# Moving the output-weight transfers four places down an in-order queue, and reordering the last iterations, in a two-problem decode attention kernel

## The chip, the cores and the metric

One core of one Trainium2 chip. The metric is the device time of one execution in microseconds (us); medians of several runs are given. A profiled execution is a run that was recorded; its "span" (first to last instruction) is mostly 1.2 to 2 us shorter than the time of the same run. The "granted clock" is the share of full speed at which TensorE was let run, as the profile gives it.

## The reference, cut to what matters

Two independent attention decodes (A and B) with the same shapes, each followed by an output projection:

```python
B, Sq, D = 2, 1, 576
Hq, Hkv, Sk, Dh = 32, 16, 16384, 128
W = 4096                                   # only the last W positions count
q = (x @ wq) -> (B, Hq, 1, Dh)
k, v = k_cache[:, :, Sk-W:], v_cache[:, :, Sk-W:]      # two query heads share a kv head
p = softmax(q k^T * Dh**-0.5);  o = p v
out = o.reshape(B, Sq, Hq*Dh) @ wo         # wo: (4096, 576)
# the outputs of A and B are concatenated on the last axis; all bf16
```

Per problem the K and V windows are 33.6 MB each and wq and wo 4.7 MB each, and every byte is used once. Nothing can be reused, so the kernel is a stream of weights and caches through the core.

## The kernel before

K and V come in slabs of 4096 KB: one slab is one batch row and four kv heads. Slabs 2G and 2G+1 (the two batch rows) make group G; there are NG = 8 groups (NSLAB = 16 slabs of K and 16 of V). The slabs pass through a ring of four slots. The wo rows of one group are a stripe of 1152 KB, in one of two buffers (`wob`). All loads are issued by SyncE, in the order of one list:

```python
        stream = []
        for t in range(NSLAB + LAG):              # LAG = 3
            if t < NSLAB:
                stream.append(("K", t))
            if t >= LAG:
                i = t - LAG
                if i % 2 == 0 and i // 2 < NG - 2:
                    stream.append(("W", i // 2))  # stripe of group G, ahead of V slab 2G
                stream.append(("V", i))
        stream.append(("W", NG - 2))
        stream.append(("W", NG - 1))
```

So the order is K0 K1 K2 K3 W0 V0 K4 V1 K5 W1 V2 K6 V3 K7 W2 V4 and so on. What a load waits for before it is issued:

```python
        def issue(key):
            kind, i = key
            if kind == "W":
                ...                               # (cut)
                sl = i % 2
                deps = [proj_op[i - 2]] if i >= 2 else []   # the buffer's last reader
                ...                               # (cut)
            r = slot_of[key]
            prior = uses[r][:uses[r].index(key)]
            deps = [last_reader[prior[-1]]] if prior else first_deps[r]  # K: transpose of slab t-2; V: PV of slab i-2
```

The iterations (t is the K slab in work; X is VectorE's transpose of half a K slab, S the score matmuls on it, PV the matmul of the probabilities with V; evac is VectorE's work on the result of a PV, dg the selection matmul that rearranges a group's result, pick what VectorE takes from it for the projection, E the output):

```python
        for t in range(NSLAB + LAG):
            i = t - LAG
            ...                                   # (cut: Gc, Gs, Gd, Gp, the groups in work)
            if live:                              # t < NSLAB
                make_X(t, 0); make_S(t, 0)
            if 0 <= i - 1 and t <= NSLAB: make_evac(i - 1)
            if Gp is not None and not last: make_pick(Gp)   # Gp = (t - 6) // 2, t even
            if Gc is not None: make_max(Gc)                 # Gc = (t - 2) // 2, t even
            ...                                   # (cut: rsum, pT of group (t - 3) // 2, t odd; Tm)
            if live:
                make_X(t, 1); make_S(t, 1)
                ...
            ...                                   # (cut: nM, sums, dg)
            if Gp is not None and not last:
                make_proj(Gp)                     # projection of group Gp with its wo stripe
                ...                               # (cut: E, at the end of a problem)
            if Gc is not None: make_bias(Gc)      # bias, then exp of the group on ScalarE
            if last: filler(4)
            if i >= 0:
                make_PV(i)
                if t >= NSLAB: make_evac(i)
        filler(3)
        make_proj(NG - 2); make_dg(NG - 1); make_pick(NG - 1)
        filler(3)
        make_proj(NG - 1); make_E(NPROB - 1)
```

The calls append to one program per engine, and each engine runs its program in order. The projection of group G-2 is in iteration t = 2G + 2, behind the second half of that iteration's scores. `filler` is a few matmuls on TensorE whose result nobody reads; they are there to keep its clock up.

## Time and profile before

| | before |
|---|---|
| time, median of 3 runs | 380.42 us (380.27 to 382.86) |
| span of the profiled run (which took 382.6 us) | 381.4 us |
| HBM to SBUF | 153.1 MB in 94.3% of the engines' time |
| transfers, 34 to 340 us | 416 GB/s |
| last bytes land | between 370 and 371 us |
| VectorE / TensorE busy | 56% / 62% |

The first line to look at is the rate row of the page: GB/s in 40 equal slices of 9.5 us.

```profile
GB/s 337 433 440 433 424 430 428 442 430 423 417 448 440 423 426 213 446 440 437 438 347 440 437 416 308 399 440 433 416 353 424 430 437 438 440 430 433 379 331 0
```

Leaving out the first and the last three, the slices are at 399 to 448, except four: 213, 347, 308 and 353. A kernel that has to bring in 153 MB and is otherwise at its full rate loses there what it never gets back. The windows view gives a hole its size. Its columns are the window, its length, busy time and number of instructions of TensorE, of its weight loads, VectorE, ScalarE and GpSimd, then the granted TensorE clock, the DMA engines' share and GB/s:

```profile
34.00:340.00 306.00, 195.00 (x998) 46.31 (x710) 194.11 (x107) 35.45 (x57) 15.45 (x56) 0.84 0.97 416
144.00:154.00 10.00, 7.49 (x61) 2.14 (x46) 4.31 (x2) 4.05 (x7) 1.06 (x3) 0.93 0.59 228
234.00:242.00 8.00, 6.12 (x58) 1.86 (x44) 3.68 (x2) 3.42 (x5) 1.06 (x3) 1.00 0.53 196
```

Over 306 us the mean is 416; the two holes shown are at 228 and 196 GB/s. The Trainium skill gives the ceiling of sixteen ports as 435 GB/s ("DMA: Bandwidth & Descriptors", section "Where 436 GB/s comes from"), and the undisturbed stretches of this trace run at 432 to 442, so the stream has little more to give than the holes. The timeline of SyncE's queue shows what stands at the end of a hole (start, length, engine and line, operation, destination and source):

```profile
119.80 0.54 SPq L369 DMA_DIRECT2D ring<-in_A_k_cache_dram  x1
149.53 0.33 SPq L353 DMA_DIRECT2D wob<-in_A_wo_dram  x1
149.91 0.54 SPq L369 DMA_DIRECT2D ring<-in_A_v_cache_dram  x1
150.49 0.61 SPq L369 DMA_DIRECT2D ring<-in_B_k_cache_dram  x1
151.54 0.54 SPq L369 DMA_DIRECT2D ring<-in_A_v_cache_dram  x1
162.56 0.54 SPq L369 DMA_DIRECT2D ring<-in_B_k_cache_dram  x1
```

From 119.80 to 149.53 us nothing is issued. Then a wo stripe goes out, and a V and a K follow at once: they had been ready, and stood behind the stripe. The Trainium skill says that any semaphore wait of a transfer takes place on the sequencer that issues it, before dispatch ("DMA: Bandwidth & Descriptors", section "Anatomy of one DMA — SWDGE (gpsimd) path"); that section is about GpSimd's transfers, but SyncE's queue agrees, as these 29.7 us without an issue show. The waits view of the queue has the stripes' line first (line waited for, us in total, times, longest):

```profile
SPq L353 <- PE tb L478: 134.3, 5, 30.2
```

134 us of waiting in five waits. The view names the small transpose on line 478, which is the next instruction after the projection on TensorE; the wait in the program is for the projection. In steady state, the distance between groups shows the pace; these are the first transposes of slabs 8, 10, 12 and 14 on VectorE:

```profile
174.04 4.45 DVE L424 STREAM_TRANSPOSE xt<-ring 128x4096 f32<-128x4096 f32 x1 [5.57 <-DMA ring<-in_B_k_cache_dram]
...
217.83 4.45 DVE L424 STREAM_TRANSPOSE xt<-ring 128x4096 f32<-128x4096 f32 x1 [3.08 <-DMA ring<-in_B_k_cache_dram]
...
262.60 4.45 DVE L424 STREAM_TRANSPOSE xt<-ring 128x4096 f32<-128x4096 f32 x1 [5.45 <-DMA ring<-in_B_k_cache_dram]
...
306.18 4.45 DVE L424 STREAM_TRANSPOSE xt<-ring 128x4096 f32<-128x4096 f32 x1 [4.39 <-DMA ring<-in_B_k_cache_dram]
```

They are 43.8, 44.8 and 43.6 us apart. The bytes of one group (four slabs and a stripe, 17.96 MB) would need 41.5 us at 433 GB/s.

Last, the end of the kernel, from the last scores on (in brackets: how long the engine had been idle, and what ended that):

```profile
345.20 0.17 DVE L511 TENSOR_REDUCE ssum<-tb 128x2 f32<-128x8 f32 x1 [5.68 <-PE tb L508]
...
350.84 1.21 DVE L458 TENSOR_REDUCE mx<-st 128x2 f32<-128x1024 f32 x1
...
357.40 1.42 ACT L488 ACTIVATE pR<-st,bias 128x512 bf16<-128x512 f32 x1 [25.44 <-DVE bias L481]
...
362.41 2.31 DVE L497 STREAM_TRANSPOSE pT<-pR 128x2048 bf16<-128x2048 bf16 x1 [1.58 <-ACT pR L488]
...
365.98 3.60 PE L527 MATMUL ot<-ring,pT 128*32 128x512 bf16 x32
...
370.99 1.91 PE L527 MATMUL ot<-ring,pT 128*32 128x512 bf16 x32
...
375.64 0.70 PE L555 MATMUL tb<-oR,selx 128*128 128x256 f32 x2
...
377.50 0.28 PE L596 MATMUL pj<-wob,oP 128*2 128x288 bf16 x1 [0.51 <-DVE oP L571]
...
380.15 0.32 SPq L610 DMA_DIRECT2D out_dram<-out_sb  x1
```

The row sums (of group 6) that follow the last scores on TensorE are read at 345.20, the maximum over the scores starts only at 350.84, exp at 357.40, and the probabilities are transposed (L497) until 364.7. The last two PVs (L527) come after that, the last one at 370.99, and the final projection at 377.50. The max is late because it stands behind the evacuation of PV 12 on VectorE, and the bias behind the projection of group 5 on TensorE.

### The profile page before, as it was taken

The numbers are of one execution on the slowest core, as the hardware profiler recorded it, in microseconds if no ns is written. First come the engines' busy times: TensorE is split into PE (matmuls) and PEld (weight loads), VectorE is DVE, ScalarE is ACT, GpSimd is POOL, SyncE is SP. The second block draws the span as 40 slices with busy tenths as digits, with TensorE's granted clock in tenths as the row PEclk, the third lists the DMA queues.
The fourth block names the chain that finished last, engine by engine and source line by source line (L and its number), as shares of the span: only waits on it lengthen the run. The fifth ranks groups of instructions, "written<-read, shape, count | busy, mean of one in ns | idle before, by whom it ended". The sixth has DMA issues, their size and how long they took to land.

```text
span 381.4 us, 2626 instructions
## 1 busy us (share of the span) xinstructions
PE 236.0 (62%) x1299; PEld 58.6 (15%) x937; DVE 212.2 (56%) x138; ACT 44.7 (12%) x77; POOL 22.0 (6%) x82
## 2 busy tenths in 40 slices
PE   0381887386546278582757768762775848754677
PEld 0110111012111112120111211110121201201122
DVE  0203889468475492907657192934839084764253
ACT  1002000500050002200050000500041000500500
POOL 3001000100100001000010001000010000000000
PEclk9997798879989968887996768888798877988769
DMA  8999999999999995999989997999989999999980
GB/s 337 433 440 433 424 430 428 442 430 423 417 448 440 423 426 213 446 440 437 438 347 440 437 416 308 399 440 433 416 353 424 430 437 438 440 430 433 379 331 0
DMA packets 6659, 153.26 MB, mean 402 GB/s; under 512 B 748, under 2 KB 888, under 8 KB 1272
## 3 DMA queue, kind: packets, MB, share of 16 engines
q1 hardware_dynamic: 6628, 153.10, 94.3%
q8 instruction: 8, 0.13, 0.1%
q14 instruction: 3, 0.02, 0.0%
q10 hardware_dynamic: 20, 0.01, 0.0%
HBM read 153.10 MB, written 0.00 MB: 401 GB/s over the span
## 4 chain that ended last, share of the span: by engine, by line
DMA 50%; DVE 22%; PE 18%; issue 7%; ACT 1%; SPq 1%; POOL 0%; DVEq 0%
DMA ring<-in_A_k_cache_dram 25%; DMA ring<-in_B_k_cache_dram 25%; DVE xt L424 13%; PE st L450 5%; PE st L242 5%; PE pj L596 2%; PE pj L242 2%; DVE oR L549 2%; DVE mx L458 2%; PE ot L527 2%; DVE tmp L548 2%; ACT pR L488 1%; DVE pT L497 1%; DVE oP L571 1%; DVE tmp L564 1%
## 5 line engine op out<-in xcount | busy, mean ns | idle before, releaser
L450 PE MATMUL st<-xt,zq 128*128 128x512 bf16 x256 | 124.1, 485 | 109.1 <-DVE xt L424 109.1
L424 DVE STREAM_TRANSPOSE xt<-ring 128x4096 f32<-128x4096 f32 x32 | 141.6, 4431 | 49.8 <-DMA ring<-in_A_k_cache_dram 27.0
L242 PE MATMUL st<-xt,zq 128*128 128x512 bf16 x256 | 122.6, 479 | 0.0
L488 ACT ACTIVATE pR<-st,bias 128x512 bf16<-128x512 f32 x32 | 40.0, 1417 | 251.4 <-DVE bias L481 251.4
L450 PEld LDWEIGHTS st<-xt,zq 128*128 128x128 bf16 x256 | 29.4, 115 | 234.1 <-DVE xt L424 125.9
L527 PE MATMUL ot<-ring,pT 128*32 128x512 bf16 x512 | 32.3, 396 | 0.0
L481 DVE SCALAR_TENSOR_TENSOR bias<-vmask,tb,offm 128x4 f32<-128x4 f32 x8 | 1.8, 225 | 43.1 <-PE tb L478 43.1
L511 DVE TENSOR_REDUCE ssum<-tb 128x2 f32<-128x8 f32 x8 | 1.3, 162 | 37.4 <-PE tb L508 37.4
L497 DVE STREAM_TRANSPOSE pT<-pR 128x2048 bf16<-128x2048 bf16 x8 | 18.4, 2304 | 2.3 <-ACT pR L488 2.3
L416 POOL TENSOR_TENSOR zq<-qs,bmask 128x64 bf16<-128x64 bf16 x32 | 8.7, 294 | 168.3 <-PE st L242 152.8
L596 PE MATMUL pj<-wob,oP 128*2 128x288 bf16 x63 | 17.3, 305 | 0.5 <-DVE oP L571 0.5
L242 PE MATMUL pj<-wob,oP 128*2 128x288 bf16 x63 | 17.3, 306 | 0.0
L549 DVE TENSOR_REDUCE oR<-tmp 128x128 f32<-128x512 f32 x16 | 16.6, 1038 | 0.6
L548 DVE SCALAR_TENSOR_TENSOR tmp<-ot,rsb,dmask 128x512 f32<-128x512 f32 x16 | 11.5, 720 | 8.0 <-PE ot L527 8.0
L527 PEld LDWEIGHTS ot<-ring,pT 128*32 128x32 bf16 x512 | 12.5, 99 | 15.6 <-issue 5.6
L252 PE MATMUL tb<-ident_b,pR 8*128 8x8 bf16 x9 | 0.7, 199 | 15.7 <-DVE pR L213 15.7
L275 PE MATMUL ot<-ring,pT 128*32 128x512 bf16 x36 | 8.9, 477 | 2.2 <-DMA ring<-in_B_wq_dram 1.7
L458 DVE TENSOR_REDUCE mx<-st 128x2 f32<-128x1024 f32 x8 | 9.7, 1213 | 0.0
L488 ACT ACTIVATION_READ_ACCUMULATOR pR<-st,bias 128x1 f32 x32 | 9.0, 281 | 0.0
L242 PE MATMUL pj<-ring,pT 128*32 128x512 bf16 x36 | 8.7, 467 | 0.0
L213 DVE TENSOR_TENSOR pR<-tmp,hmask 8x1152 bf16<-8x1152 bf16 x1 | 1.3, 1347 | 12.7 <-DMA tmp<-in_B_x_dram 12.7
L555 PE MATMUL tb<-oR,selx 128*128 128x256 f32 x16 | 6.1, 466 | 3.3 <-DVE ssum L511 3.3
(57 smaller groups left out, 61.0 us busy)
## 6 DMA issues: line engine op xcount, KB each, us to landing
ring<-in_A_k_cache_dram SPq DMA_DIRECT2D x8, 4096.0 KB, 29.4
ring<-in_A_v_cache_dram SPq DMA_DIRECT2D x8, 4096.0 KB, 32.0
ring<-in_B_k_cache_dram SPq DMA_DIRECT2D x8, 4096.0 KB, 27.2
ring<-in_B_v_cache_dram SPq DMA_DIRECT2D x7, 4096.0 KB, 27.4
ring<-in_A_wq_dram SPq DMA_DIRECT2D x1, 4608.0 KB, 13.6
ring<-in_B_wq_dram SPq DMA_DIRECT2D x1, 4608.0 KB, 24.0
wob<-in_A_wo_dram SPq DMA_DIRECT2D x4, 1152.0 KB, 15.8
wob<-in_B_wo_dram SPq DMA_DIRECT2D x3, 1152.0 KB, 5.3
```

The source lines that it names most:

```text
L242: return e.add_instruction(mybir.InstMatmult(name=nc.get_next_instruction_name(), engine=mybir.EngineType.PE, ins=[e.lower_ap(mv_), e.lowe ...
L275: last = e.matmul(o, wt, mv_, start=first, stop=True, skip_group_check=True)
L416: last = e.tensor_tensor(dst, src, msk, ALU.mult)
L424: Xop[(t, jh)] = dve(lambda e: e.transpose(xt[:, jh, :].bitcast(FP32).rearrange("p (kp x kt) -> p x kp kt", kp=2, kt=2), ring[:, r, jh * H ...
L450: last = e.matmul(ob, wt, mv_, start=first, stop=True, skip_group_check=True)
L458: ch[(G, "max")] = dve(lambda e: e.tensor_reduce(mx[:], st[:, :].rearrange("p (x t) -> p t x", t=2), AX.X, ALU.max), [Sop[(2 * G + 1, 1)]] ...
L488: last = e.activation(pR[:].rearrange("p (x k) -> p k x", k=4)[:, kv, :], st[:, :].rearrange("p (x t) -> p t x", t=2)[:, kv % 2, :], ACTF.Exp,
L497: pT_op[G] = dve(lambda e: e.transpose(pT[:, v, :].rearrange("p (w j q) -> p j w q", w=4, q=8), pR[:].rearrange("p (j w q) -> p j w q", w= ...
L527: last = e.matmul(OTB[32 * c:32 * c + 32, :], pT[:, v, base + 32 * c:base + 32 * c + 32], ring[:, r, jj * 128:(jj + 4) * 128], start=rd == ...
L548: evac_op[i] = dve(lambda e: e.scalar_tensor_tensor(tv, o, rsb[:, v, b:b + 1], dm, ALU.mult, ALU.mult), deps, "ev%d" % i)
L549: ch[(G, "red%d" % b)] = dve(lambda e: e.tensor_reduce(oR[:, b, :], tmp[:].rearrange("p (j d) -> p d j", j=4), AX.X, ALU.add), [evac_op[i] ...
L596: e.matmul(PJ[0], wt, wob[:, v, j, 0:NH], start=start and j == 0, stop=True, skip_group_check=True)
```

## The change

The intent: let a stripe never be what the queue waits for, by queueing it one group later (ahead of the even V slab of the following group), and let the chain max, bias, exp, transpose of the last group follow its last scores directly.

```diff
                 i = t - LAG
-                if i % 2 == 0 and i // 2 < NG - 2:
-                    stream.append(("W", i // 2))
+                if i % 2 == 0 and 0 < i // 2 < NG - 1:
+                    stream.append(("W", i // 2 - 1))
                 stream.append(("V", i))
@@ (cut: the loop now ends with t = NSLAB - 1 = T; its conditions for later t are dropped)
+            if t == T:
+                make_max(NG - 1)
+                make_pick(Gd)
             if i >= 0:
                 make_PV(i)
-                if t >= NSLAB:
-                    make_evac(i)
+        i = T - LAG
+        make_Tm_pe(NG - 1)
+        make_nM(NG - 1)
+        make_evac(i)
+        make_bias(NG - 1)
+        make_PV(i + 1)
+        make_evac(i + 1)
+        make_proj(NG - 3)
+        make_dg(NG - 2)
+        make_pick(NG - 2)
+        make_rsum(NG - 1)
+        make_pT(NG - 1)
+        make_sums(NG - 1)
+        filler(4)
+        make_PV(i + 2)
+        make_evac(i + 2)
+        make_PV(i + 3)
+        make_evac(i + 3)
         filler(3)
         make_proj(NG - 2)
         make_dg(NG - 1)
```

The stream becomes K5 W0 V2 K6 V3 K7 W1 V4 and so on. Bytes and matmuls are the same as before.

More of the change, by code (lines that the diff above doesn't have):

```diff
@@ L614, in build_kernel @@
             make_Z(t)
-        for t in range(NSLAB + LAG):
+        T = NSLAB - 1
+        for t in range(NSLAB):
             i = t - LAG
             odd = t % 2 == 1
-            live = t < NSLAB
             Gc = (t - 2) // 2 if not odd and t >= 2 else None
@@ L622, in build_kernel @@
             Gp = (t - 6) // 2 if not odd and t >= 6 else None
-            if Gc is not None and Gc >= NG:
-                Gc = None
-            if Gs is not None and Gs >= NG:
-                Gs = None
-            last = t == NSLAB + LAG - 1
-            if live:
-                make_X(t, 0)
-                make_S(t, 0)
-            if 0 <= i - 1 and t <= NSLAB:
+            make_X(t, 0)
+            make_S(t, 0)
+            if i >= 1:
                 make_evac(i - 1)
-            if Gp is not None and not last:
+            if Gp is not None:
                 make_pick(Gp)
@@ L641, in build_kernel @@
                 make_Tm_pe(Gc)
-            if live:
-                make_X(t, 1)
-                make_S(t, 1)
-                if t + 2 < NSLAB:
-                    make_Z(t + 2)
+            make_X(t, 1)
+            make_S(t, 1)
+            if t + 2 < NSLAB:
+                make_Z(t + 2)
             if Gc is not None:
@@ L652, in build_kernel @@
                 make_dg(Gd)
-                if Gd == NG - 2:
-                    make_pick(Gd)
-            if Gp is not None and not last:
+            if Gp is not None:
                 make_proj(Gp)
@@ L660, in build_kernel @@
                 make_bias(Gc)
-            if last:
-                filler(4)
+            if t == T:
+                make_max(NG - 1)
+                make_pick(Gd)
             if i >= 0:
                 make_PV(i)
-                if t >= NSLAB:
-                    make_evac(i)
+        i = T - LAG
[16 more added lines that the diff above has]
+        make_evac(i + 3)
         filler(3)
```

## The prediction

> **What bounds the kernel now.** The transfers. In stretches without a stall (34 to 146, 154 to 190, 198 to 234, 242 to 278, 286 to 346 us; windows view) 432 to 442 GB/s arrive. The Trainium skill ("DMA: Bandwidth & Descriptors", section "Where 436 GB/s comes from") gives 435 GB/s as the ceiling of the sixteen ports; this trace agrees. The 153 MB at 433 GB/s take 354 us (my division) of the 381.4 us span. The rest:
>
> 1. Four holes: in 144-154, 190-198, 234-242 and 278-286 us the rate is 228, 346, 196 and 318 GB/s. Against 433 that is 4.7 + 1.6 + 4.4 + 2.1 = 12.8 us lost.
> 2. The end: the last bytes land at about 370.3 us, 11 us before the end.
> 3. A start of 2 to 3 us.
>
> **Why the holes.** In the timeline of the SyncE queue every hole ends with the issue of a wo stripe (149.5, 192.9, 238.2, 281.4 us), with a V, a K and a V right after it: the queue is in order, and the stripe held them back. The stripe of group G waits for the projection of G-2, at the end of iteration 2G+2, when only one K slab (9.7 us) is still in flight.
>
> **What the change moves.** Bytes and matmuls stay equal. The stripe is queued two transfers later, behind K(2G+5), when that projection is long done. The next waits in that queue (a V for a PV, a K for a transpose) come, as I count it, 15 to 20 us before their transfer's turn. So I expect no new hole, and the stripe still lands before its projection.
>
> Would compute bind? In VectorE's timeline two iterations take about 39 us where they hardly wait for a transfer (129.3 to 168.3; 306.2 to 345.4); one group's transfers take 17.96 MB / 433 GB/s = 41.5 us. DMA still binds, by 2 to 3 us. Groups (first transposes at 174.0, 217.8, 262.6, 306.2) were 43.6 to 44.8 us apart and should be 41 to 42.
>
> **The end.** Before, the last scores end at 344.9, exp starts at 357.4, pT ends at 364.7, and the last two PVs follow. Reordered, exp should start about 6 us after the scores (max 1.2, pool operations, PV 1.9, nM, bias), so pT is done before the last V lands. Estimate: K15 lands at 312, scores end at 331, pT at 345, last V cut at 353, last byte at 357.5 (370.3 less 12.8). What remains is part of evac, projection 6, dg and pick 1.9, projection 7 with its output 3.9: the end is 6 to 8 us after the last byte, not 11. TensorE will idle waiting for V15, so the last matmuls may run at granted clock 0.50 (the trace shows it after idle stretches, as "TensorE: Matmul & The Clock Gate", section "What's actually happening", says); projection 6 would take 3.9 instead of 2.0 us.
>
> **Sum.** 12.8 us of holes and 3 to 5 us of tail: 380.4 - 15.5 = about 365 us. Range 361.5 to 370. Faster by over 2%: 0.93; within 2%: 0.065; slower by over 2%: 0.005.
>
> **What would show it.** No slice of the rate row under about 400 GB/s between first and last; no long wait of a stripe before its issue; group distance 41 to 42 us; last byte near 357.5; exp of the last group within about 7 us of its scores.
>
> **What would make it wrong.** Jitter in the 39 us compute chains that two K slots don't absorb, so that small holes appear; another wait taking the stripe's place in the queue; cold matmuls or a late last stripe (it waits for projection 5, now later on TensorE) in the tail.

## The result, and the profile after

| | before | after |
|---|---|---|
| time, median of 4 runs | 381.34 us (380.27 to 382.86) | 368.30 us (366.13 to 370.06) |
| ratio | 1 | 0.9652 (95% interval 0.9587 to 0.9718) |
| span of the profiled run | 381.4 us | 364.9 us |
| transfers, 34 to 340 us | 416 GB/s | 431 GB/s |
| last bytes land | between 370 and 371 us | between 359 and 360 us |
| from there to the end | about 11 us | about 5.5 us |

Ratios are the mean time of one kernel's runs over that of the other's runs of the same rounds, so not quite the ratio of the medians quoted. The profiled run of after is the fastest of its four (366.13 us), and that of before was a slow one (382.6 us), so the two spans differ by more (16.5 us) than the medians (13.0 us); why the others are up to 4 us slower is taken up below.

The rate row of after:

```profile
GB/s 324 449 432 417 445 418 445 420 442 427 433 417 453 413 453 392 451 435 432 427 418 449 413 449 408 449 427 438 424 422 436 427 438 419 441 431 431 413 415 128
```

Between the first slice and the last ones none is below 392. The same windows:

```profile
34.00:340.00 306.00, 202.55 (x1100) 49.83 (x796) 200.65 (x119) 39.73 (x66) 17.32 (x63) 0.86 1.00 431
144.00:154.00 10.00, 6.76 (x54) 1.91 (x43) 8.26 (x5) 5.01 (x8) 0.58 (x2) 0.87 1.03 443
234.00:242.00 8.00, 3.94 (x16) 0.77 (x8) 7.96 (x5) 1.57 (x4) 0.20 (x1) 1.00 1.01 434
```

431 over the whole stretch, and the former holes cannot be told from the rest. The queue:

```profile
118.86 0.54 SPq L369 DMA_DIRECT2D ring<-in_A_k_cache_dram  x1
119.44 0.59 SPq L353 DMA_DIRECT2D wob<-in_A_wo_dram  x1
125.79 0.54 SPq L369 DMA_DIRECT2D ring<-in_A_v_cache_dram  x1
139.19 0.53 SPq L369 DMA_DIRECT2D ring<-in_B_k_cache_dram  x1
147.24 0.54 SPq L369 DMA_DIRECT2D ring<-in_A_v_cache_dram  x1
```

The stripe is issued in the same microsecond as the K slab ahead of it: it no longer waits, and the next V waits instead, at 125.79, for a PV. That wait costs nothing, since V3, K7 and a stripe, issued before, are still in flight then (K6 has just landed, and K7 lands 20 us later). The waits view has the stripes' line with one wait left, that of the last stripe for projection 5, in the tail:

```profile
SPq L369 <- PE ot L527: 86.4, 12, 9.0
...
SPq L353 <- PE pj L242: 11.2, 1, 11.2
```

The pace, at the same four transposes:

```profile
168.14 4.45 DVE L424 STREAM_TRANSPOSE xt<-ring 128x4096 f32<-128x4096 f32 x1 [3.71 <-DMA ring<-in_B_k_cache_dram]
...
209.78 4.45 DVE L424 STREAM_TRANSPOSE xt<-ring 128x4096 f32<-128x4096 f32 x1 [4.99 <-DMA ring<-in_B_k_cache_dram]
...
251.43 4.45 DVE L424 STREAM_TRANSPOSE xt<-ring 128x4096 f32<-128x4096 f32 x1 [2.26 <-DMA ring<-in_B_k_cache_dram]
...
293.08 4.45 DVE L424 STREAM_TRANSPOSE xt<-ring 128x4096 f32<-128x4096 f32 x1 [2.39 <-DMA ring<-in_B_k_cache_dram]
```

41.6 to 41.7 us apart, which is what the bytes alone take (17.96 MB at 431 GB/s are 41.7 us). VectorE now waits 2.3 to 5.0 us for each of these slabs: it is the side with time to spare. The end:

```profile
330.93 0.17 DVE L511 TENSOR_REDUCE ssum<-tb 128x2 f32<-128x8 f32 x1 [5.68 <-PE tb L508]
...
331.21 1.20 DVE L458 TENSOR_REDUCE mx<-st 128x2 f32<-128x1024 f32 x1
...
336.13 1.41 ACT L488 ACTIVATE pR<-st,bias 128x512 bf16<-128x512 f32 x1 [18.82 <-DVE bias L481]
...
341.14 2.31 DVE L497 STREAM_TRANSPOSE pT<-pR 128x2048 bf16<-128x2048 bf16 x1 [0.45 <-ACT pR L488]
...
344.49 3.60 PE L527 MATMUL ot<-ring,pT 128*32 128x512 bf16 x32 [1.69 <-DMA ring<-in_B_v_cache_dram]
...
357.13 0.28 PE L596 MATMUL pj<-wob,oP 128*2 128x288 bf16 x1 [0.81 <-DMA wob<-in_B_wo_dram]
...
359.19 0.70 PE L555 MATMUL tb<-oR,selx 128*128 128x256 f32 x2
...
361.05 0.28 PE L596 MATMUL pj<-wob,oP 128*2 128x288 bf16 x1 [0.51 <-DVE oP L571]
...
363.69 0.32 SPq L610 DMA_DIRECT2D out_dram<-out_sb  x1
```

The maximum starts at 331.21, within 0.3 us of the row sums; exp at 336.13; the transpose is done at 343.4, and PV 14 waits for its V slab (L527 at 344.49, released by a DMA). What is left after the last bytes is projection 6, the selection matmul (L555), the pick, projection 7 and the store.

### The profile page after: what moved, and what is told of

Read it like the earlier page. It is cut to its first block, busy times and chain, and to the rows that moved or that the text cites. A ratio compares the mean times of both kernels' runs of the same rounds, so it can differ in the third digit from the quotient of the medians.

```text
span 364.9 us, 2628 instructions
## 1 busy us (share of the span) xinstructions
PE 230.3 (63%) x1297; PEld 57.4 (16%) x937; DVE 211.7 (58%) x138; ACT 44.8 (12%) x77; POOL 21.9 (6%) x82
## 4 chain that ended last, share of the span: by engine, by line
DMA 60%; DVE 23%; PE 7%; issue 6%; ACT 1%; SPq 1%; POOL 0%
DMA ring<-in_B_k_cache_dram 31%; DVE xt L424 14%; DMA ring<-in_A_k_cache_dram 14%; DMA wob<-in_B_wo_dram 8%; DMA ring<-in_B_wq_dram 7%; DVE oR L549 2%; PE st L450 2%; DVE mx L458 2%; DVE pT L497 2%; PE st L242 2%; PE pj L242 1%; ACT pR L488 1%; DVE tmp L548 1%; PE pj L596 1%; DVE oP L571 1%
## 5 line engine op out<-in xcount | busy, mean ns | idle before, releaser
L450 PE MATMUL st<-xt,zq 128*128 128x512 bf16 x256 | 120.9, 472 | 98.3 <-DVE xt L424 98.3
L242 PE MATMUL st<-xt,zq 128*128 128x512 bf16 x256 | 119.7, 468 | 0.0
L527 PE MATMUL ot<-ring,pT 128*32 128x512 bf16 x512 | 34.1, 411 | 4.8 <-DMA ring<-in_B_v_cache_dram 4.8
L596 PE MATMUL pj<-wob,oP 128*2 128x288 bf16 x63 | 15.7, 286 | 1.3 <-DMA wob<-in_B_wo_dram 0.8
L527 PEld LDWEIGHTS ot<-ring,pT 128*32 128x32 bf16 x512 | 12.7, 100 | 22.0 <-DMA ring<-in_B_v_cache_dram 8.3
L242 PE MATMUL pj<-wob,oP 128*2 128x288 bf16 x63 | 15.8, 286 | 0.0
L275 PE MATMUL ot<-ring,pT 128*32 128x512 bf16 x36 | 8.9, 486 | 5.2 <-DMA ring<-in_B_wq_dram 4.7
L607 ACT ACTIVATE out_sb<-pj 2x288 bf16<-2x288 f32 x2 | 0.8, 399 | 58.2 <-PE pj L242 36.1
## 6 DMA issues: line engine op xcount, KB each, us to landing
wob<-in_A_wo_dram SPq DMA_DIRECT2D x4, 1152.0 KB, 30.2
```

What stands on the lines that cost most here:

```text
L242: return e.add_instruction(mybir.InstMatmult(name=nc.get_next_instruction_name(), engine=mybir.EngineType.PE, ins=[e.lower_ap(mv_), e.lowe ...
L275: last = e.matmul(o, wt, mv_, start=first, stop=True, skip_group_check=True)
L450: last = e.matmul(ob, wt, mv_, start=first, stop=True, skip_group_check=True)
L527: last = e.matmul(OTB[32 * c:32 * c + 32, :], pT[:, v, base + 32 * c:base + 32 * c + 32], ring[:, r, jj * 128:(jj + 4) * 128], start=rd == ...
L596: e.matmul(PJ[0], wt, wob[:, v, j, 0:NH], start=start and j == 0, stop=True, skip_group_check=True)
```

## The experiments

All ran beside the kernel before on the same chip; 0.5% is about what three to five rounds can tell. The theory was: (1) the holes are the queue blocked by a stripe that waits for its projection, while the transfers in flight run out; (2) the reordered tail saves some us at the end. Rivals: the tail makes most of the gain; or it is not the wait but the place of the stripe's bytes in the stream.

### Each part alone

The first part alone: only the three lines of `stream`.

> Before, with the wo stripes queued two transfers later and the old order of the last iterations. My theory (the holes are the queue blocked by a stripe that waits for a projection): the four holes vanish, X of slab 15 starts at 312 to 314 us as in the changed kernel, and the old tail of 54.5 us from there (326.8 to 381.4 in before) gives a span of 366 to 368 us: about 14 us less than before, ratio 0.962 to 0.970, 2 us behind the changed kernel. Rival (the gain is mostly the reordered tail): the span stays above 375 us.

Measured: 368.97 us median of 6 runs, ratio 0.9664 (0.9626 to 0.9703), span 367.5. The transpose of slab 15 started at 313.53, the last bytes landed between 359 and 360 us, and the end followed 8 us later. As expected, and the rival (most of the gain from the tail) falls.

The second part alone: only the lines of the loop and of the tail.

> Before, with the new order of the last iterations and the stripes where they were. My theory: the four holes stay (group distance 43 to 45 us), the last byte stays near 370.5 us, and the end follows it by 5.7 us as in the changed kernel: span about 376 us, 5 us less than before, ratio 0.984 to 0.990. Then the two parts don't add up (14 + 5 against 16.5 together), because both shorten the same tail. Rival (tail is most of the gain): span under 370 us.

Measured: 378.69 us, ratio 0.9923 (0.9887 to 0.9959), span 377.4; the rate from 34 to 340 us was 417 GB/s, so the holes stayed. The gain was smaller than expected: the end came 8 us after the last bytes (369 to 370 us), not 5.7. In the timeline, projection 6 ran at half speed; these are its first and its last matmul but one, and the selection matmul that had to wait for it:

```profile
367.40 0.40 PE L596 MATMUL pj<-wob,oP 128*2 128x288 bf16 x1 [1.32 <-DMA wob<-in_B_wo_dram]
...
370.71 0.44 PE L596 MATMUL pj<-wob,oP 128*2 128x288 bf16 x1
...
371.33 1.06 PE L555 MATMUL tb<-oR,selx 128*128 128x256 f32 x2
```

A matmul each 0.24 us instead of each 0.12: sixteen take 3.9 us instead of 2.0. This is the cold TensorE that the prediction had named as a risk. In the profiled run of the changed kernel it had not happened.

The changed kernel again, for comparison:

> The changed kernel again, as a measure for the others on this chip: 366 to 370 us, ratio 0.96 to 0.97, span 365 to 367.

Measured: 368.20 us, ratio 0.9652 (0.9616 to 0.9688), span 365.0. So the parts don't add up: in the spans, 13.9 us for the stripes and 4.0 for the order make 17.9, and together they give 16.5. These are single runs; in the medians of the times it is 12.1 and 2.4 against 12.9 together. The shortfall of 1.4 to 1.6 us is no more than one kernel's runs differ among themselves, so it is likely and not shown. In the medians, the order is worth 2.4 us without the stripes' move and 0.8 with it, which the intervals can't tell from nothing. (The profiled run of the order alone was the slowest of its six; the shortest span of the six was 375.1 us.)

### Is it the wait or the place?

One transfer later instead of four (the expectation says two), on top of the changed kernel:

```diff
-                if i % 2 == 0 and 0 < i // 2 < NG - 1:
-                    stream.append(("W", i // 2 - 1))
                 stream.append(("V", i))
+                if i % 2 == 0 and i // 2 < NG - 2:
+                    stream.append(("W", i // 2))
```

> The changed kernel with each stripe queued one transfer later than in before (right behind the even V slab), not two. My theory (a hole opens only if the data in flight run out before the projection): when the even iteration starts, V, K and one V slab (29 us) are in flight ahead of the stripe, and the projection ends after about 20 us, so one step is enough: no hole, span 364 to 367 us, ratio 0.962 to 0.970, the same as the changed kernel within 0.5%. Rival (it is the distance of two transfers, or bytes of the stripe ahead of V and K, that counts): about half of the gain, ratio 0.975 to 0.99.

Measured: 367.04 us, ratio 0.9618 (0.9576 to 0.966), span 365.0. In the queue the stripes still wait (they are issued at 148.10, 189.82, 233.00 and 274.47 us, each followed at once by a K slab that stood behind it), but one more V slab is in flight meanwhile, and the rate from 34 to 340 us is 431 GB/s (the stripes' line of the waits view, where 30.2 us was the longest wait before, and the windows view):

```profile
SPq L353 <- PE tb L478: 81.2, 4, 22.5
34.00:340.00 306.00, 203.46 (x1094) 49.84 (x795) 198.82 (x117) 37.54 (x64) 17.32 (x63) 0.85 1.00 431
```

A wait in the queue without a hole: what counts is whether the data in flight outlast it.

The stripes where they were, but the projection earlier. In even iterations, `make_proj(Gp)` moves from its old place to ahead of `make_X(t, 1)`, on top of before:

```diff
+            if Gp is not None and live:
+                make_proj(Gp)
+                if (Gp + 1) % GP == 0:
+                    make_E(Gp // GP)
             if live:
                 make_X(t, 1)
@@ (cut: the call in the old place stays for t >= NSLAB alone)
```

> Before, with the stripes where they were and the old tail, but with the projection of each even iteration moved ahead of the second half of the scores on TensorE; that half waits some 4 us for its transpose anyway. The projection then ends about 10 to 12 us after the start of the iteration instead of 20. My theory (the wait for the projection makes the hole): the stripe is issued while a K slab is still in flight, the holes shrink from 12.8 us in total to under 2 us, span 367 to 370 us, ratio 0.962 to 0.975, near the run with only the stripes moved. Rival (the place of the stripe's bytes in the stream makes the loss): holes and time as before, ratio over 0.99.

Measured: 371.40 us, ratio 0.9723 (0.9689 to 0.9757), span 370.2. The third stripe was issued at 142.61 instead of 149.53, and the windows view has no hole left:

```profile
34.00:340.00 306.00, 203.60 (x1048) 48.70 (x752) 196.74 (x112) 35.35 (x57) 15.36 (x56) 0.82 1.00 431
144.00:154.00 10.00, 5.13 (x46) 1.53 (x39) 5.32 (x4) 4.99 (x8) 1.26 (x4) 0.97 1.02 433
```

So the wait makes the loss, not the place: with the bytes in the old place and the wait shortened, the rate is that of the changed kernel. The span is just over the expected range, and that part does belong to the place: with no stripe moved behind it, the last K slab lands later (slab 15 is transposed at 315.45, against 313.53 with the stripes moved), and the old tail takes 54.7 us from there.

The wait made worse: one transfer earlier than before, ahead of the odd K slab.

```diff
+            if t >= LAG and (t - LAG) % 2 == 0 and (t - LAG) // 2 < NG - 2:
+                stream.append(("W", (t - LAG) // 2))
             if t < NSLAB:
                 stream.append(("K", t))
             if t >= LAG:
-                i = t - LAG
-                if i % 2 == 0 and i // 2 < NG - 2:
-                    stream.append(("W", i // 2))
-                stream.append(("V", i))
+                stream.append(("V", t - LAG))
```

> Before, with each stripe queued one transfer earlier (ahead of the odd K slab): the suspected wait made worse. My theory: only one V slab (9.7 us) is then in flight while the projection is 20 us away, and the K slab of the next iteration waits as well; each of the four groups from the third on takes about 54 us instead of 44, so 415 to 440 us, with holes of over 10 us each. Rival (bytes of the stripe in the wrong place): no change, 380 us.

Measured: 424.25 us, one run (so of unknown state), span 422.7. The rate row, in slices of 10.6 us:

```profile
GB/s 336 447 422 434 445 412 443 437 410 448 419 431 403 2 310 447 425 416 104 257 416 431 447 150 161 447 443 406 242 82 435 440 443 436 409 447 440 403 374 2
```

Four holes again, at the same four stripes, each now spread over two slices and worth 12.3 to 13.5 us (the missing GB/s of both against 431, times 10.6 us). The first lasts from 137 to 151 us; the groups are 54.7 us apart on average (transposes at 164.46, 219.02, 273.70 and 328.65). One slab of 9.7 us less in flight made each group some 11 us longer. Two other ways to take the wait away were not run: a third stripe buffer, and issuing the stripes from another engine's queue.

### What sets the end

In the changed kernel, projection 6 on TensorE stands between the last evacuation (done at 356.8 us) and the selection matmul (359.19), which the final projection needs. The swap (it also drops three filler matmuls):

```diff
         filler(3)
-        make_proj(NG - 2)
         make_dg(NG - 1)
         make_pick(NG - 1)
-        filler(3)
+        make_proj(NG - 2)
         make_proj(NG - 1)
```

> The changed kernel with the selection matmul and the pick of the last group ahead of projection 6 on TensorE, and without the filler between them. My theory of the tail (the last stripe pair and the last evac are ready at 357.1 and 356.8 us, and projection 6 delays the selection matmul from 356.9 to 359.2): the end comes 1.5 to 2 us earlier, span about 363 us. Rival (the landing of the last stripe binds): less than 0.5 us.

Measured: 367.13 us, ratio 0.9613 (0.9577 to 0.9649), span 363.4: 1.6 us less in the profiled runs, 1.1 in the medians of the same chip (367.13 against 368.20). The intervals overlap; the pair with fillers below, whose runs hardly differ, decides it. The selection matmul started at 357.01.

The runs of the changed kernel lie between 366 and 370 us, which is wide beside 1 us. Next, fillers before each piece of the last PV (its V slab comes in three transfers), on top of the swap:

```diff
             for c0, c1, dma in stream_dma[("V", i)]:
                 deps = [dma, pT_op[G], evac_op[i - 1] if i >= 1 else q_ev[0]]
+                if i == NSLAB - 1:
+                    filler(4)
                 PVop[i] = pe(pv_moving(i, c0, c1), deps, "PV%d_%d" % (i, c0))
```

> The run with the selection matmul ahead of projection 6, plus four filler matmuls before each of the three pieces of the last PV, to keep TensorE's clock up while it waits for the last V slab. If half clock in the tail costs anything in the usual run, PV 15 and the two projections run at full clock: 0 to 2 us less than with the swap alone, ratio 0.956 to 0.961. If the tail is bound by the landing of the last bytes: no difference, 0.961.

Measured: 364.85 us, ratio 0.9558 (0.9531 to 0.9584), and all six runs within 364.80 to 365.04. The span was 363.6, no better than the 363.4 of the swap's profiled run: the fillers don't shorten the best run, they make every run the best one. To see whether the clock does that alone, the same fillers without the swap, with the two others on the same chip:

> The changed kernel with four filler matmuls before each of the three pieces of the last PV, nothing else. So far the changed kernel spread over 366.1 to 370.1 us from run to run, and the run with swap and fillers over 364.8 to 365.0. If the spread is half clock on TensorE in the tail (projection 6 in 3.9 instead of 2.0 us, as in the run with only the order changed), the fillers close it: all runs within 0.6 us of one another, near 366.3. Rival (the spread comes from the transfers or the start): the spread stays at 2 us or more.

Measured: 366.15 us, ratio 0.9598 (0.9562 to 0.9633), six runs within 366.05 to 366.31.

> The run with swap and fillers, again, on the same chip as the next two: 364.8 to 365.1 us, 1.3 to 1.6 us under the changed kernel with fillers, 3 us under the changed kernel.

Measured: 364.91 us, ratio 0.9564 (0.9525 to 0.9603), 364.74 to 365.03; 1.2 us under the changed kernel with fillers.

> The changed kernel for comparison on this chip: median 367 to 369 us, spread of 2 us or more.

Measured: 366.62 us, a little under what was expected, ratio 0.962 (0.958 to 0.9661), and 366.04 to 368.63: a spread of 2.6 us. This time the profiled run was a slow one (368.12 us, span 366.9). The windows view of that run, around the last PV and projection 6 (the granted clock is the third number from the end):

```profile
353.00:357.00 4.00, 3.29 (x19) 0.51 (x17) 1.77 (x2) 0.00 (x0) 0.00 (x0) 0.50 1.01 416
357.00:361.00 4.00, 3.70 (x16) 0.96 (x8) 0.00 (x0) 0.00 (x0) 0.00 (x0) 0.50 0.42 162
```

The same windows with the fillers:

```profile
353.00:357.00 4.00, 2.88 (x23) 0.52 (x18) 1.74 (x2) 0.00 (x0) 0.00 (x0) 1.00 1.00 413
357.00:361.00 4.00, 3.40 (x21) 1.06 (x11) 1.07 (x3) 0.00 (x0) 0.00 (x0) 1.00 0.43 164
```

At a clock of 0.50 TensorE gets through 16 instructions from 357 to 361 us, at 1.00 through 21. Projection 6 takes 3.9 us in the first and 2.0 us in the second, and the span differs by just that (366.9 and 364.9). The Trainium skill describes the two clock states, the return to half rate after an idle window of some 3.4 us and the free-running phase of that window ("TensorE: Matmul & The Clock Gate", section "What's actually happening"); 0.50 and 1.00 and the change from run to run agree with it. TensorE waits here for the pieces of V15, and whether its clock is still low when stripe 6 lands differs from run to run: in the profiled run of after it was 0.61 over 353 to 357 us and 1.00 from 357 to 361. How long the idle window is, no run here measures.

The version with swap and fillers beats both kernels: 364.9 us against 366.6 and 381.5 on the same chip.

## Why the prediction was right

The measured median, 368.3 us, lies in the range of 361.5 to 370 and on the slow side of the 365 foreseen; "faster by over 2%" (0.93) came true. Point by point:

- **The queue blocked by a stripe.** Shown. Moving the stripe (one or four places) or bringing its projection forward both closed the holes (431 GB/s in each case), and moving it the other way deepened them by about the one slab (9.7 us) that was no longer in flight.
- **"Two transfers later".** A miscount: it is four. It did no harm, since one place is already enough.
- **No new wait in the stripe's place.** Right: there are waits (86.4 us of V slabs for PVs in the waits view), but the data in flight outlast them. One slice of the rate row was at 392, where the prediction had said none under about 400.
- **Compute has 2 to 3 us to spare per group.** Right, if a little low: groups are 41.6 to 41.7 us apart, and VectorE waits 2.3 to 5.0 us for each even slab.
- **12.8 us of holes.** Mis-sized. The last bytes came 11 us sooner, and over 34 to 340 us the rate rose from 416 to 431 GB/s, which is 10.7 us ((431 - 416) / 431 of 306 us). The holes themselves were measured well: outside the four windows of the prediction, before ran at 434 GB/s ((306 x 416 less the 9,160 that the windows hold) over 272 us). But that rate was not kept: the changed kernel and the three other runs without holes that were looked at (stripes only, one transfer later, early projection) all streamed at 431. Why it is 431 and not 434 is not settled.
- **3 to 5 us of tail, on top of the holes.** About right as a difference between the two spans (11 to about 5.5 us after the last bytes), but it is not the worth of the reordering, which is 2.5 us in the profiled runs once the stripes are moved and 0.8 us in the medians. With the old order the end is a chain of 54.0 to 54.7 us from the transpose of slab 15 (before 54.6, stripes only 54.0, early projection 54.7), so it moved ahead with that slab, and more than the last bytes did. With the new order the last bytes set the end: slab 15 was transposed at 312.53 in the changed kernel and at 315.42 with the stripe one place later, and both spans were 365.
- **Cold matmuls in the tail.** Named as a risk, with the right size (3.9 instead of 2.0 us), and left to the range. It is what most of the distance between the fastest run (366.1) and the slower ones rests on: with fillers the spread fell from 2.6 to 0.3 us. That both states occur in one kernel was not foreseen.
- **The last stripe late.** Did not happen: in the profiled run projection 7 waited for the pick, not for its stripe. (Projection 6 waited 0.8 us for its own.)
- **Luck in the sum.** The last bytes were foreseen at 357.5 us and landed 2 us later; the end was foreseen 6 to 8 us after them and came, in the profiled run, after about 5.5. The two misses cancel in that run, not in the colder ones. The sum itself takes off 15.5 us, less than its own two terms (12.8 and 3 to 5); the medians differ by 13.0.

The 16 runs of the changed kernel fall into two groups: seven spans of 364.8 to 365.1 us and nine of 366.7 to 367.5, some 2 us apart, as one cold projection makes them. That every long one has this cause is not shown; one of them was read in its profile. The slowest time, 370.06 us, has a span of 367.2, so it lies 2.9 us above its span where the others lie 1.2 to 2.0 above theirs.

What stays open: what fills the 1.2 to 2.9 us outside the span.

## What to carry to other kernels

In an in-order queue, put a transfer behind everything that can go before its condition is met, and judge a wait there by what is still in flight when it begins, not by its length: one slab less in flight cost 11 us a group, and waits of up to 22.5 us for a projection, with one slab more in flight, left no hole. When two changes shorten the same end, measure each alone and both together before crediting either. If a time is bimodal by 2 us, look at the TensorE clock in the last few microseconds before blaming the change: a dozen matmuls without a reader made every run a fast one.

## What the Trainium skill lacked or had wrong

- "DMA: Bandwidth & Descriptors", section "Where 436 GB/s comes from", says that for HBM to SBUF the limit of about 358 GB/s per core binds. Here one core brought in 431 GB/s over 306 us from HBM. The sentence leaves out a condition that the page has elsewhere: the note under its table of measured rates (425 at 16 MB) gives them for a core whose neighbour is idle, and the 358 for two that stream.
- "TensorE: Matmul & The Clock Gate" describes the free-running window, and puts the ramp at under 1% of a typical span and not worth fitting. It does not say that a wait near the end makes a kernel's time bimodal: 366.04 to 368.63 us in one kernel, and 366.05 to 366.31 with fillers in that wait. The 2 us are about 0.5% of the time, so the page's figure stands. The page says to warm up before a benchmark and to avoid idle gaps; filler matmuls in a wait are not on it.
- "Perfetto Trace Analysis", section "Optimization Strategy", reads a repeating gap on the saturated engine as a possible lack of buffers. Here the same gap, four times, was closed with the same two buffers by moving the transfer in the queue (416 to 431 GB/s). No page that was consulted treats the order of transfers in one issuing queue as a cause.
